# A new order of the instructions, sums by batch ahead of the experts' layers, and 20 products of zeros on TensorE

## The chip, the cores and the metric

The kernel runs on one core of a Trainium2 chip. The metric is the device time of one execution in microseconds (us). The core has four engines that compute, each with its own queue of instructions in program order: TensorE (PE in the rows; PEld is its loading of weights), VectorE (DVE), ScalarE (ACT) and GpSimd (POOL). SyncE (SP) issues the large DMA transfers.

## The reference

An attention with 32 inducing points over four batches of 11456 rows of 128 numbers, and behind it a soft mixture of eight experts with four slots each. Cut to what matters:

```python
def mab(q, kv):
    s = scale * (q @ kv.transpose(0, 2, 1))
    a = softmax(s, -1)
    return a @ kv
h = mab(I, x)                        # 32 x 128 for each batch
x = mab(x, h).reshape(B * N, D)
logits = x @ phi                     # 45824 x 32
slot_input = softmax(logits, 0).T @ x        # over ALL rows of all batches
for e in range(E):
    slot_out[e] = relu(slot_input[e] @ w1[e]) @ w2[e]
out = softmax(logits, 1) @ slot_out
```

The softmax over axis 0 runs over every row of every batch, so the experts' layers can't start until the last row has its logits, and no output can be written until the experts' layers are done.

## The kernel before, in words

The rows are cut into 24 tiles (`n` = 0 to 23, six for each batch), each 128 partitions of 15 rows with 32 scores a row, so a tile of scores is 128 x 480. A tile goes through these steps:

- loads `xn` (rows on the partitions) and `xt` (transposed); for batch 0 `xt` is made on TensorE.
- `first_scores`, `first_max`, `first_sum`, `first_out`: the first attention of a batch, tiles `s1p`, `s`, `e`, `ha`, `h`.
- `second(n)`: the second attention's scores `s2p`, moved to SBUF by DVE (`bts`, tile `bt`), the maximum (`bmx`, tile `bm`), the subtraction on POOL (`bsb`), the exponential on ACT (`bxp`), transposes `tt`, the logits `lp`, and their scaled copy in `l_all` (`ble`, `blf`). POOL scales `bt` by 1/sum (`bml`).
- `segment(k)`: three tiles form one of eight segments (`SEGS`). `h0` (or `blm` for single tiles) takes the column maximum of their logits, `h1` to `h4` spread it over the partitions (tiles `pt`, `mc`, `pb`, and `m_all`), `ds` subtracts it (tile `d`, on DVE for tiles listed in `DV`, on POOL for the others), `de` takes the exponential, and `c2` sums into `u`, 128 x 32 for each segment, which `u1` copies to `us_all`.
- `experts()`: the sums of all segments are brought to one maximum and put through the experts. In `before` the first seven segments are joined early (`e1` to `e7`) and the last one late (`g1` to `g8`). `e5` multiplies each segment's sum with its batch's `h` (tile `sip`). `g9` are the first layer's products (tile `hpm`), `ga`, `gb`, `gc` the relu and the transpose, `gd` the second layer (tile `so`), `ge`, `gf`, `gs` bring the result, divided by the total `rz`, to `srs`. That total comes from POOL (`g4b`, `g4c`, tiles `vs` and `vr`) through a product on TensorE (`g7`, tile `zpp`).
- `third(n)`: the softmax over the 32 columns (`cm`, `ct`, `cz`), which needs no expert, and its transposed copy into `l_all` (`ctr`). `ml` (row `ct<-ct,cz`) is its scaling on POOL, `sb` its subtraction, `hf` a half sum.
- `output(n)`: the products with `srs` (tile `po`), copies to `ot` by ACT or DVE, and the store.

The work of every tile is listed in a `Plan`, but the order in which it is issued is the table `ORDER`, two characters for each operation; it fixes each engine's queue and also in which order buffers of a ring (`RINGS`) are reused. The costs given to `op(...)` don't act on the chip. PSUM tiles come from one ring `mm` of eight.

Of the kernel before, what the change touches and what calls it, by code (L numbers as in the profile page):

```python
# [1063 lines left out]
```

## Time and profile before

| | |
|---|---|
| median of 3 runs | 225.55 us (225.12 to 226.31) |
| profiled execution: its own time | 225.43 us |
| its span, first to last instruction | 223.3 us |
| busy: PE, DVE, ACT, POOL | 189.0, 162.1, 138.1, 124.9 us |
| mean granted TensorE clock | 0.920 of full speed |
| read from and written to HBM | 49.84 MB, 23.59 MB |

Of the profiled execution's time 2.1 us lie outside its span. Busy times are unions of an engine's instructions; a busy TensorE need not be at its peak, since its matmuls overlap.

### The profile page before, as it was taken

How to read it: one execution, taken by the hardware profiler on the slowest of the kernel's cores; microseconds unless marked ns; L12 is line 12 of the kernel's file. 1: busy time of each engine (PE TensorE's matmuls, PEld its weight loads, DVE VectorE, ACT ScalarE, POOL GpSimd, SP SyncE). 2: the span in 40 equal slices, each digit the busy share in tenths (PEclk: the TensorE clock that was granted, in tenths of full speed). 3: DMA queues.
4: the chain of work that ended last, by engine and by line, in shares of the span. 5: the costliest groups of instructions: out<-in, count | busy, mean ns of one | idle time of the engine just before them, and what ended most of it. 6: DMA issues, size and time to landing. Idle time of an engine off the chain costs nothing. (4 is left out here: it accounts for less than half of the span.)

```text
span 223.3 us, 6826 instructions
## 1 busy us (share of the span) xinstructions
PE 189.0 (85%) x2762; PEld 126.0 (56%) x2762; DVE 162.1 (73%) x368; ACT 138.1 (62%) x371; POOL 124.9 (56%) x135
## 2 busy tenths in 40 slices
PE   8899999999999999999998996899879989960000
PEld 8666563687356986348884695788635543510000
DVE  0113867987999989998989899946799999762000
ACT  2587433966465994458966697613299999991000
POOL 0000001586488968588697899977968857610000
PEclk9999999999999999999999999557999999995555
DMA  7999999995999999899999920000079999999994
GB/s 222 406 424 416 418 413 399 422 416 209 312 398 423 414 417 414 302 388 420 414 416 417 409 95 3 0 3 4 4 290 409 417 418 413 415 413 420 421 412 204
DMA packets 12846, 73.87 MB, mean 331 GB/s; under 512 B 1680, under 2 KB 2832, under 8 KB 12816
## 3 DMA queue, kind: packets, MB, share of 16 engines
q1 hardware_dynamic: 12384, 73.27, 81.3%
q8 instruction: 22, 0.36, 0.6%
q10 hardware_dynamic: 432, 0.17, 0.3%
q14 instruction: 8, 0.07, 0.1%
HBM read 49.84 MB, written 23.59 MB: 329 GB/s over the span
## 5 line engine op out<-in xcount | busy, mean ns | idle before, releaser
L941 PE MATMUL po<-l_all,srs 32*128 32x480 f32 x192 | 35.8, 609 | 5.1 <-DVE ot L952 2.8
L952 ACT COPY ot<-po 128x480 f32<-128x480 f32 x67 | 35.1, 679 | 2.8 <-PE po L941 2.8
L568 POOL TENSOR_TENSOR bt<-bt,bm 128x480 f32<-128x480 f32 x24 | 23.7, 1000 | 16.4 <-DVE bm L564 8.1
L941 PEld LDWEIGHTS po<-l_all,srs 32*128 32x128 f32 x192 | 17.2, 183 | 23.1 <-DVE ot L952 10.7
L913 POOL TENSOR_TENSOR ct<-ct,cz 128x480 f32<-128x480 f32 x24 | 23.8, 994 | 6.2 <-DVE cz L532 5.9
L620 POOL TENSOR_TENSOR bt<-bt,bz 128x480 f32<-128x480 f32 x24 | 23.6, 995 | 5.2 <-DVE bz L602 2.7
L326 DVE TENSOR_SCALAR_CACHE_REDUCE s<-s1p 128x480 f32<-128x480 f32 (+1 forms) x24 | 15.2, 644 | 15.5 <-PE s1p L315 15.2
L590 PE MATMUL lp<-bdg,a2t 128*128 128x132 f32 x192 | 25.8, 280 | 0.1
L505 POOL TENSOR_TENSOR ct<-l_all,cm 128x512 f32<-128x512 f32 x20 | 21.0, 1052 | 8.5 <-DVE l_all L916 6.7
L691 POOL TENSOR_TENSOR d<-l_all,m_all 128x512 f32<-128x512 f32 x20 | 22.9, 1166 | 4.4 <-ACT m_all L670 3.2
L590 PEld LDWEIGHTS lp<-bdg,a2t 128*128 128x128 f32 x192 | 23.2, 190 | 3.7 <-ACT a2t L584 1.6
L391 PE MATMUL ha<-xn,e 128*32 128x128 f32 x600 | 21.0, 275 | 0.0
L315 PE MATMUL s1p<-xt,it_sb 128*32 128x480 f32 x160 | 19.9, 573 | 0.7 <-ACT xt L300 0.7
L315 PE MATMUL s2p<-xt,hts 128*32 128x480 f32 x160 | 19.0, 572 | 1.0 <-issue 1.0
L509 ACT ACTIVATE ct<-ct 128x480 f32<-128x480 f32 x24 | 15.7, 661 | 6.6 <-POOL ct L505 5.5
L391 PEld LDWEIGHTS ha<-xn,e 128*32 128x32 f32 x600 | 16.9, 110 | 2.9 <-issue 2.0
L952 DVE COPY ot<-po 128x480 f32<-128x480 f32 x29 | 17.9, 634 | 0.2 <-PE po L941 0.2
L694 ACT ACTIVATE d<-d 128x512 f32<-128x512 f32 x24 | 14.9, 630 | 5.0 <-POOL d L691 2.5
L372 ACT ACTIVATE s<-s,negm 128x480 f32<-128x480 f32 (+1 forms) x24 | 16.4, 685 | 2.4 <-DVE negm L357 2.4
L328 POOL MEMSET s<- 128x16 f32 x4 | 0.5, 113 | 31.1 <-DVE e L375 30.8
L916 DVE STREAM_TRANSPOSE l_all<-ct 128x480 f32<-128x480 f32 x24 | 15.7, 661 | 2.3 <-POOL ct L913 2.3
L561 DVE STREAM_TRANSPOSE bt<-s2p 128x480 f32<-128x480 f32 x24 | 15.7, 666 | 1.7 <-PE u L704 0.9
(126 smaller groups left out, 370.3 us busy)
## 6 DMA issues: line engine op xcount, KB each, us to landing
xn<-xn SPq DMA_DIRECT2D x19, 960.0 KB, 11.6
out<-ot SPq DMA_DIRECT2D x19, 960.0 KB, 8.5
xt<-xt SPq DMA_DIRECT2D x14, 960.0 KB, 14.8
w<-w SPq DMA_DIRECT2D x8, 960.0 KB, 10.7
l_all<-xn SPq DMA_DIRECT2D x4, 960.0 KB, 10.3
l_all<-xt SPq DMA_DIRECT2D x4, 960.0 KB, 13.5
out<-ot SPq DMA_DIRECT2D x6, 480.0 KB, 7.3
out<-ot SPq DMA_DIRECT2D x8, 240.0 KB, 2.5
```

The source lines that it names most:

```text
L315: nc.tensor.matmul(dst[32 * g : 32 * g + 32, :w], lhs, src, start=True, stop=True)
L372: nc.scalar.activation(t[:, :v], t[:, :v], AF.Exp, bias=T["negm", b, g], accum_out=z6[:, a : a + 1])
L391: nc.tensor.matmul(ha[32 * q : 32 * q + 32, :P], T["e1", a][:, j * S : (j + 1) * S], T["xn", a][:, j * P : (j + 1) * P], start=c == lo and ...
L505: nc.gpsimd.tensor_tensor(t.rearrange("p (a e s) -> p a e s", s=S, e=2), l_blocks(n), m, op=ALU.subtract)
L509: nc.scalar.activation(t, t, AF.Exp)
L568: nc.gpsimd.tensor_tensor(t, t, T["bm", n][:, :nb].unsqueeze(2).broadcast_to(full), op=ALU.subtract)
L590: nc.tensor.matmul(pt[:, q * 4 * SZ : (q * 4 + m) * SZ], t[: m * S, q * P : (q + 1) * P], bdgs[b % 2].rearrange("p q s -> p (q s)")[: m * ...
L620: nc.gpsimd.tensor_tensor(t, t, T["bz", n][:, :nb].unsqueeze(2).broadcast_to(full), op=ALU.mult)
L691: e.tensor_tensor(t.rearrange(o, s=S, e=2), l_pairs(n), m, op=ALU.subtract)
L913: nc.gpsimd.tensor_tensor(t, t, T["cz", n][:, :nb].unsqueeze(2).broadcast_to([P, nb, S]), op=ALU.mult)
L941: nc.tensor.matmul(ptile("mm", ("po", 4 * n + g))[:, :w], T["srs",][q, :], l_of(n)[q, :], start=True, stop=True)
L952: (nc.vector.tensor_copy if dve else nc.scalar.copy)(ot[:, g * w : (g + 1) * w], T["po", m][:, :w])
```

## The change

The constants and the code of the changed parts, cut:

```diff
-CHALF = [9, 10, 11, 16]
+CHALF = [9, 10, 11, 12, 16]
 CQ = []
 CB = []
-DV = [12, 20, 21, 23]
+DV = [12, 20, 21, 22, 23]
...
-OD2 = [0, 2, 3, 4, 5, 6, 7, 8, 9, 10, 11, 12, 13, 14, 15, 16, 17, 18, 20, 22, 23]
+OD2 = [0, 2, 3, 4, 5, 7, 8, 9, 10, 11, 12, 13, 14, 16, 17, 18, 20, 21, 22, 23]
...
-NTAG = {3: 'xe', 4: 'xd', 5: 'xc', 18: 'xa'}
-SPLIT = {0: 1, 1: 1, 2: 4, 3: 2, 22: 2, 23: 4, 10: 2}
+NTAG = {3: 'xe', 4: 'xd', 5: 'xc', 18: 'xa', 1: 'xa'}
+SPLIT = {0: 4, 1: 1, 2: 4, 3: 2, 22: 2, 23: 4, 10: 2, 21: 2}
...
+NF = 20
...
+    "000102030406050e070a08090p0b0c0f0d0h0g0A0j0i0l0k0q0w0m0s0r0u0L0t0n0v0x0B0o0y0C0W0H0z0D0F170E180M0G190Q0N3z1a0O0I0S1f0X1i0Z1g130Y1j113D0P1h100R1k120J0T3H140U1l0K1m150V3E163L3A1b1c3I"
...
+K = sum(t < (B - 1) * NCH for t in SEG_AT)
...
-    def warm(key, count):
+    def warm_into(t, count=1):
         for _ in range(count):
-            nc.tensor.matmul(T[key][:, :P], wz, wz, start=True, stop=True)
+            nc.tensor.matmul(t[:, :P], wz, wz, start=True, stop=True)
...
-        K = NSEG - 1
-        last = slice(K * S, NSEG * S)
-        m_last = m_all[:, K * S : (K + 2) * S]
-        m_past = m_all[:, (K + 1) * S :]
+        m_last = m_all[:, K * S :]
+        m_past = m_all[:, NSEG * S :]
+        last = slice((NSEG - 1) * S, NSEG * S)
+        W = NSEG + 1 - K
...
+            o = 4 * ZW + K * S
+            T["ws",] = mb[:, 4 * ZW : o]
+            T["uss",] = mb[:, o : o + K * S]
+            T["usp",] = mb[:, o + K * S : o + (K + B - 1) * S]
...
+        def e6(b):
+            def f():
+                lo, hi = (min(t for t in range(K + 1) if SEG_AT[t] >= NCH * x) for x in (b, b + 1))
+                nc.vector.tensor_reduce(T["usp",][:, b * S : (b + 1) * S], T["uss",][:, lo * S : hi * S].rearrange("p (k s) -> p s k", s=S), axis=AX.X, op=ALU.add)
+            return f
+
...
         def e5():
             sip = ptile("mm", ("sip",))
-            for t in range(K):
-                nc.tensor.matmul(sip[:, :S], T["h", SEG_AT[t] // NCH], T["uss",][:, t * S : (t + 1) * S], start=t == 0, stop=t == K - 1)
+            for b in range(B - 1):
+                nc.tensor.matmul(sip[:, :S], T["h", b], T["usp",][:, b * S : (b + 1) * S], start=b == 0, stop=b == B - 2)
...
-            nc.vector.tensor_reduce(stile("vs", ("vs",), S, 1), T["uss",].rearrange("p (k s) -> p s k", s=S), axis=AX.X, op=ALU.add)
+            nc.vector.tensor_reduce(stile("vs", ("vs",), S, 1), T["usp",].rearrange("p (k s) -> p s k", s=S), axis=AX.X, op=ALU.add)
...
-                blocks(stile("w2", ("wl",), 2 * S, 1)), blocks(m_last), T["nm",].unsqueeze(1).broadcast_to([P, 2, S]), op=ALU.subtract,
+                blocks(stile("w2", ("wl",), W * S, 1)), blocks(m_last), T["nm",].unsqueeze(1).broadcast_to([P, W, S]), op=ALU.subtract,
...
+        def g4a():
+            r = slice(K * S, (NSEG - 1) * S)
+            nc.gpsimd.tensor_tensor(us_all[:, r], us_all[:, r], T["wl",][:, : (W - 2) * S], op=ALU.mult)
+
+        def g4d(k):
+            def f():
+                nc.gpsimd.tensor_tensor(T["vs",], T["vs",], us_all[:, k * S : (k + 1) * S], op=ALU.add)
+            return f
 
...
+        def g6c():
+            for k in range(K, NSEG - 1):
+                nc.tensor.matmul(T["sit",][:, :S], T["h", B - 1], us_all[:, k * S : (k + 1) * S], start=False, stop=False)
...
+        for b in range(B - 1):
+            op("DVE", 0.2, ("e6", b), e6(b), [("uss",), ("mb",)], [("usp", b)])
+        op("PE", 0.3 * (B - 1), ("e5",), e5, [("mb",)] + [(x, b) for b in range(B - 1) for x in ("usp", "h")], [("sip",)], [("mm", ("sip",))], ni=4 * B - 4)
...
+        op("Pool", 0.25 + 0.06 * (W - 2), ("g4a",), g4a, [("wl",)], [("us", k) for k in range(K, NSEG - 1)])
         op("PE", 0.4, ("g6a",), g6a, [("sis",)], [("sit",)], [("mm", ("sit",))], ni=4)
-        op("DVE", 0.1, ("g5",), g5, [("u", K), ("wl",)], [("us", K)])
...
+    def fill(k):
+        def f():
+            warm_into(ptile("mm", ("fill", k)))
+        return f
+
+    for k in range(NF):
+        op("PE", 0.22, ("fill", k), fill(k), [("eps0",)], [("fill", k)], [("mm", ("fill", k))], ni=4)
     T["plan"] = plan
```

`K` is 6 in place of 7: the early join takes the six segments of batches 0 to 2, and the late one the two segments of batch 3. The early sums are added by batch on DVE (`e6`, three instructions, tile `usp` inside `mb`), so `e5` has three products in place of seven. The late join gains a scaling on POOL (`g4a`), an addition on POOL (`g4d`) and a product (`g6c`). Tile 22's subtraction `ds` moves from POOL to DVE, tile 12's third softmax gains a half sum on POOL, the first tile's store is cut otherwise, the load of tile 1 goes to another buffer. Each of the 20 fills is one 128 x 128 product of zeros into a PSUM tile of its own that nobody reads. All other lines of the diff change costs given to `op(...)`, and `ORDER` is a new table.

What the new table does is seen in the queues. On TensorE, from the last segment's maximum (`pb`) to the sums `sit` that feed the experts, the queue before is:

```order
L667 MATMUL pb_2369<-cst,mc_2348 128x32
L772 MATMUL sip<-mb,h_513 128x32 x2
L772 MATMUL sip<-mb,h_1056 128x32 x2
L772 MATMUL sip<-mb,h_1431 128x32 x2
L772 MATMUL sip<-mb,h_2053 128x32
L704 MATMUL u_2404<-d_2376,bt_2057 32x32 x15
L704 MATMUL u_2404<-d_2378,bt_2096 32x32 x15
L704 MATMUL u_2404<-d_2393,bt_2105 32x32 x15
L803 MATMUL sit<-sis,cst 128x32
```

and of the changed kernel (`u_2330` is the sum of segment 6, `u_2427` that of segment 7):

```order
L669 MATMUL pb_2380<-cst,mc_2371 128x32
L225 MATMUL fill_2388<-srs 128x128
L706 MATMUL u_2330<-d_2320,bt_2003 32x32 x15
L225 MATMUL fill_2409<-srs 128x128
L782 MATMUL sip<-mb,h_509 128x32
L782 MATMUL sip<-mb,h_916 128x32
L782 MATMUL sip<-mb,h_1437 128x32
L225 MATMUL fill_2425<-srs 128x128
L706 MATMUL u_2427<-d_2406,bt_2061 32x32 x15
L225 MATMUL fill_2451<-srs 128x128
L822 MATMUL sit<-sis,cst 128x32
L706 MATMUL u_2427<-d_2417,bt_2073 32x32 x15
```

Eleven fills stand ahead of these rows, two of them directly ahead of `pb`, and two stand behind the last `sit`, ahead of `hpm`; the three `sip` products are behind the last `u` products of segment 6 and ahead of those of segment 7, as the seven were.

On DVE, at the last tiles' scores `bts` (`bt<-s2p`), the queue before is (`t_5` is the maximum of segment 5 by `h0`):

```order
L561 STREAM_TRANSPOSE bt_2010<-s2p_1977 128x480
L652 TENSOR_REDUCE t_5_2020<-l_all 128x32
L564 TENSOR_REDUCE bm_2051<-bt_2010 128x15
L561 STREAM_TRANSPOSE bt_2057<-s2p_2005 128x480
L462 TENSOR_TENSOR bdg_89<-gp_2041,cst 128x4x32
L564 TENSOR_REDUCE bm_2074<-bt_2057 128x15
L561 STREAM_TRANSPOSE bt_2096<-s2p_2015 128x480
L561 STREAM_TRANSPOSE bt_2105<-s2p_2046 128x480
L564 TENSOR_REDUCE bm_2113<-bt_2096 128x15
L564 TENSOR_REDUCE bm_2122<-bt_2105 128x15
```

and of the changed kernel:

```order
L563 STREAM_TRANSPOSE bt_2061<-s2p_1987 128x480
L563 STREAM_TRANSPOSE bt_2073<-s2p_1998 128x480
L566 TENSOR_REDUCE bm_2080<-bt_2061 128x15
L566 TENSOR_REDUCE bm_2090<-bt_2073 128x15
L563 STREAM_TRANSPOSE bt_2097<-s2p_2065 128x480
L654 TENSOR_REDUCE t_5_2115<-l_all 128x32
L604 RECIPROCAL bz_2125<-bz_2125 128x15
L566 TENSOR_REDUCE bm_2133<-bt_2097 128x15
```

The maximum `t_5` and one reciprocal moved behind the last `bt<-s2p` and ahead of the last `bm<-bt`.

On POOL, ahead of `vr`, which the total of the softmax waits for, the queue before is:

```order
L517 TENSOR_TENSOR ch_2580<-ct_2533 128x240
L913 TENSOR_TENSOR ct_2490<-ct_2490,cz_2531 128x480
L792 TENSOR_TENSOR vs<-vs,wl 128x32
L517 TENSOR_TENSOR ch_2627<-ct_2548 128x240
L795 TENSOR_TENSOR vr<-vs,us_all 128x128
```

and of the changed kernel:

```order
L811 TENSOR_TENSOR vs<-vs,wl 128x32
L942 TENSOR_TENSOR ct_2495<-ct_2495,cz_2531 128x480
L807 TENSOR_TENSOR vs<-vs,us_all 128x32
L519 TENSOR_TENSOR ch_2587<-ct_2541 128x240
L507 TENSOR_TENSOR ct_2593<-l_all,cm_1925 128x512
L507 TENSOR_TENSOR ct_2629<-l_all,cm_2282 128x512
L519 TENSOR_TENSOR ch_2642<-ct_2593 128x240
L942 TENSOR_TENSOR ct_2541<-ct_2541,cz_2599 128x480
L519 TENSOR_TENSOR ch_2676<-ct_2629 128x240
L814 TENSOR_TENSOR vr<-vs,us_all 128x128
```

Between `vs<-vs,wl` and `vr` there was one half sum `ch`; now there are three, two subtractions `ct<-l_all`, two scalings `ct<-ct` and the new addition.

## Rows read from the trace of the kernel before

**Rows 1.** The page's slices: granted TensorE clock, DMA share, DMA rate, 40 equal slices.
```profile
PEclk9999999999999999999999999557999999995555
DMA  7999999995999999899999920000079999999994
GB/s 222 406 424 416 418 413 399 422 416 209 312 398 423 414 417 414 302 388 420 414 416 417 409 95 3 0 3 4 4 290 409 417 418 413 415 413 420 421 412 204
```
**Rows 2.** Windows: busy time (instructions) of PE, PEld, DVE, ACT, POOL; clock; DMA share, GB/s.
```profile
135.00:140.00 5.00, 3.15 (x147) 2.34 (x149) 5.00 (x12) 3.86 (x11) 5.00 (x6) 1.00 0.01 3
140.00:145.00 5.00, 4.04 (x74) 3.71 (x66) 4.82 (x11) 3.14 (x8) 4.78 (x7) 0.50 0.00 0
...
150.00:155.00 5.00, 5.00 (x113) 4.32 (x109) 2.55 (x6) 1.56 (x4) 4.92 (x7) 0.64 0.01 3
165.00:170.00 5.00, 3.79 (x28) 1.89 (x21) 5.00 (x12) 5.00 (x13) 2.68 (x3) 1.00 1.04 389
```
**Rows 3.** Windows of longer stretches, same columns.
```profile
35.00:140.00 105.00, 101.91 (x1769) 69.52 (x1769) 97.47 (x216) 72.60 (x217) 80.20 (x82) 1.00 0.87 349
163.00:163.50 0.50, 0.50 (x6) 0.33 (x3) 0.50 (x2) 0.50 (x2) 0.50 (x2) 1.00 0.63 223
163.50:220.50 57.00, 32.94 (x173) 15.61 (x170) 34.95 (x70) 37.78 (x88) 23.69 (x24) 0.83 1.01 412
```
**Rows 4.** Chain of waits from the last sums to srs: start, us, what.
```profile
142.59 3.19 PE sip L772 x14
145.79 1.43 PE u L704 x90
...
148.55 5.72 PE hpm L826 x112
...
156.70 2.38 PE so L855 x80
...
160.24 0.35 DVE srs L868
```
**Rows 5.** Timeline of PE at the kernel's start: start, us, what, idle before.
```profile
1.11 3.78 PE L223 MATMUL warm<-srs 128*128 128x128 f32 x16 [1.11 <-DVE srs L219]
```
**Rows 6.** Timeline of DVE, three places.
```profile
55.98 1.74 DVE L652 TENSOR_REDUCE t<-l_all 128x32 f32<-128x1536 f32 x1
...
127.36 0.68 DVE L561 STREAM_TRANSPOSE bt<-s2p 128x480 f32<-128x480 f32 x1 [0.91 <-PE u L704]
127.97 1.17 DVE L564 TENSOR_REDUCE bm<-bt 128x15 f32<-128x480 f32 x2
```
**Rows 7.** Timeline of ACT, the last segment's exponentials.
```profile
143.11 1.88 ACT L694 ACTIVATE d<-d 128x512 f32<-128x512 f32 x3 [0.82 <-DVE d L691]
```
**Rows 8.** Timeline of POOL, 130 to 158 us.
```profile
130.63 2.90 POOL L620 TENSOR_TENSOR bt<-bt,bz 128x480 f32<-128x480 f32 x3
133.49 5.64 POOL L691 TENSOR_TENSOR d<-l_all,m_all 128x512 f32<-128x512 f32 x5
139.09 0.66 POOL L759 TENSOR_TENSOR mb<-m_all 128x224 f32<-128x224 f32 x1
...
143.61 0.32 POOL L781 TENSOR_TENSOR wl<-m_all,nm 128x64 f32<-128x64 f32 x1
...
144.82 1.29 POOL L746 MEMSET ma<- 128x1440 f32 x1
...
149.16 1.05 POOL L505 TENSOR_TENSOR ct<-l_all,cm 128x512 f32<-128x512 f32 x1 [1.14 <-DVE l_all L916]
150.17 0.99 POOL L913 TENSOR_TENSOR ct<-ct,cz 128x480 f32<-128x480 f32 x1
...
154.91 0.25 POOL L792 TENSOR_TENSOR vs<-vs,wl 128x32 f32<-128x32 f32 x1
156.52 0.70 POOL L517 TENSOR_TENSOR ch<-ct 128x240 f32<-128x240 f32 x1 [1.36 <-DVE cz L526]
157.18 0.46 POOL L795 TENSOR_TENSOR vr<-vs,us_all 128x128 f32<-128x128 f32 x1
```

More of the change, by code (lines that the diff above doesn't have):

```diff
@@ L872, in experts @@
         op("Pool", 1.15, ("g0b",), g0b, [wk[2][0]], [("z2", 1), ("ws",), ("uss",)], [("x", ("mb",))])
-        op("DVE", 0.3, ("e1",), e1, [("mk", k) for k in range(K)], [("mp",)])
+        op("DVE", 0.33, ("e1",), e1, [("mk", k) for k in range(K)], [("mp",)])
         op("Pool", 0.6, ("e2",), e2, [("mp",), ("mb",)] + [("mk", k) for k in range(K)], [("ws",)])
@@ L876, in experts @@
         op("Pool", 0.6, ("e4",), e4, [("ws",), ("mb",)] + [("us", k) for k in range(K)], [("uss",)])
-        op("PE", 0.3 * K, ("e5",), e5, [("uss",), ("mb",)] + [("h", SEG_AT[k] // NCH) for k in range(K)], [("sip",)], [("mm", ("sip",))], ni=4 * K)
-        op("DVE", 0.3, ("e7",), e7, [("uss",), ("mb",)], [("vs",)])
-        op("DVE", 0.1, ("g1",), g1, [("mk", K), ("mp",)], [("nm",)])
-        op("Pool", 0.3, ("g2",), g2, [("nm",), ("mk", K), ("mp",)], [("wl",)])
-        op("ACT", 0.14, ("g3",), g3, [], [("wl",)])
@@ L882, in experts @@
-        op("DVE", 0.09, ("g4",), g4, [("wl",), ("sip",)], [("sis",)])
+        for b in range(B - 1):
+            op("DVE", 0.2, ("e6", b), e6(b), [("uss",), ("mb",)], [("usp", b)])
+        op("PE", 0.3 * (B - 1), ("e5",), e5, [("mb",)] + [(x, b) for b in range(B - 1) for x in ("usp", "h")], [("sip",)], [("mm", ("sip",))], ni=4 * B - 4)
+        op("DVE", 0.2, ("e7",), e7, [("mb",)] + [("usp", b) for b in range(B - 1)], [("vs",)])
+        op("DVE", 0.15, ("g1",), g1, [("mk", k) for k in range(K, NSEG)] + [("mp",)], [("nm",)])
@@ L883, in experts @@
+        op("Pool", 0.35, ("g2",), g2, [("nm",), ("mp",)] + [("mk", k) for k in range(K, NSEG)], [("wl",)])
+        op("ACT", 0.16, ("g3",), g3, [], [("wl",)])
+        op("DVE", 0.11, ("g4",), g4, [("wl",), ("sip",)], [("sis",)])
+        op("Pool", 0.25 + 0.06 * (W - 2), ("g4a",), g4a, [("wl",)], [("us", k) for k in range(K, NSEG - 1)])
         op("PE", 0.4, ("g6a",), g6a, [("sis",)], [("sit",)], [("mm", ("sit",))], ni=4)
-        op("DVE", 0.1, ("g5",), g5, [("u", K), ("wl",)], [("us", K)])
@@ L901, in experts @@
                 op("PE", 0.244 * len(es), ("gd", k, es[0]), gd(k, es), [("z2", k), ("ma",), ("mb",)] + wk[2], [("so",)], [] if k or es[0] else [("mm", ("so",))], ni=16 * len(es))
[L902 removed]
+        op("DVE", 0.21, ("ge",), ge, [("so",)], [("sos",)])
         op("PE", 0.4, ("gf",), gf, [("sos",)], [("sr",)], [("mm", ("sr",))], ni=4)
[L904 removed]
+        op("DVE", 0.26, ("gs",), gs, [("sr",), ("rz",)], [("srs",)])
     def third(n):
```

94 lines of the change are left out of this document (46 added, 48 removed).

## The prediction

> **What bounds the kernel now.** I read the slices first: the DMA is full while the inputs come in, idle for some 33 us in the middle, and full again to the end [rows 1]. The last stretch is a drain: from 163.5 to 220.5 us the DMA share is 1.01 at 412 GB/s [rows 3], which is 23.5 of the 23.59 MB written. No engine can shorten it. The kernel's end is therefore the first store plus a constant. The first store's data start to move between 163.0 and 163.5 [rows 3], behind `srs`, which ends at 160.24 + 0.35 = 160.59 us [rows 4]. A microsecond won ahead of `srs` is a microsecond of the kernel, as long as the copies keep ahead of the drain; ACT and DVE, which make them, are busy 37.78 and 34.95 of its 57 us [rows 3], so there is room. All of the change is judged by when `srs` ends.
>
> The chain of waits says what lies ahead of it [rows 4]: `sip` from 142.59, the last `u`, the experts' first layer `hpm` from 148.55, the second layer `so` to 156.70 + 2.38 = 159.08, and 1.51 us from there to the end of `srs`. Much of that ran at half clock: the granted clock is 1.00 up to 140 us, 0.50 from there, and in 150 to 155 us it averages 0.64 [rows 2], so it was back at 1.00 for (0.64 - 0.50) / 0.50 = 28% of that window, from about 153.6. These are TensorE's levels of 2.4 and 1.2 GHz. The price is visible in the products themselves: `hpm` took 5.72 / 112 = 51 ns each, nearly all at half clock, `so` 2.38 / 80 = 29.8 ns at full [rows 4]. Ahead of the fall, in 135 to 140, PE was busy 3.15 of 5 us [rows 2]. In the long stretch before, 35 to 140 us, DVE is the engine to watch: busy 97.47 of 105 us, idle 7.53, while POOL has 24.8 us idle [rows 3].
>
> **Sums by batch.** Seven `sip` products show as 14 records, 3.19 us, 228 ns a record at half clock [rows 4]. Three products are six records: 1.4 us at half clock, 0.7 at full. They stand ahead of the last `u`, so up to 2.5 us could come off, but the last `u` also need the last three exponentials, which end at 143.11 + 1.88 = 144.99 [rows 7]. That caps it at about 0.8 us (145.79 against 144.99), and the DVE queue decides what of it is left, below. The three additions on DVE have no row of before; by the smallest and the largest neighbour, a `bm` maximum of 480 numbers at 1.17 / 2 = 0.58 us [rows 6] bounds one from above, zero from below; for 64 numbers I take 0.2, and they lie in the wait between `mc` and the last `pb`, where before two `cm` maxima lay.
>
> **The fills.** At the kernel's start the same product of zeros took 3.78 / 16 = 236 ns a record [rows 5]. A fill is two records: 0.47 us at that price, 0.24 if that stretch ran at half clock, which the slices don't show. `so` against `hpm` differ by a factor of 51 / 29.8 between the two levels, so I take 0.24, and 20 are 4.7 us of PE. Where they stand PE was waiting (1.85 us in 135 to 140 alone [rows 2]). Two stand ahead of `hpm`, 0.47 us, where PE waits for the copy `ma` anyway; their cost is between 0 and 0.47, and I take 0.1. If that cover is gone, it is 0.47. What they can buy is the clock. With it held, 128 records of `hpm` take 128 x 29.8 = 3.8 us against 5.72 + 16 x 29.8 ns = 6.2 before.
>
> Does the clock hold? Ahead of the fall PE was busy 3.15 of 5 us; in 165 to 170 it was busy 3.79 and the clock stayed at 1.00 [rows 2]. The nine fills that now stand in the former stretch are 2.1 us of PE work, as much as the 1.85 us that were idle, and eight more (1.9 us) are strewn through 140 to 147.5, where the real work at full clock is some 4 us. No row tells what is enough; I take it that the clock holds as the likelier. The Trainium skill speaks against part of this: its page "TensorE: Matmul & The Clock Gate", section "A second HAM failure mode: psum-queue depth-cycling", tells of a kernel whose clock swung because PE idled in small gaps between groups of products. By that page the small gaps that remain between fills would still cost the clock, which is the third case below; the fall at 140 here agrees with it, since no wait of PE ahead of it was a long one (1.85 us in all, in several pieces).
>
> **From the last scores to hpm.** On DVE the last `bt<-s2p` ends at 127.36 + 0.68 = 128.04 [rows 6]. I leave that time where it is: counted through the two queues, DVE has ahead of it one `bm` (0.58) and three `cm` (0.6 each, estimated from `bm`) more and one segment maximum (1.74 [rows 6]) less, +0.6 us, and one first score maximum more (480 numbers, 0.6 too) is done in the first 33 us, where DVE waits, so the two cancel. Behind it, up to the last segment's `mc`, the segment maximum is new, and one `bm` and one `cm` are gone: +0.5 us. The last exponential began at 144.99 - 1.88 / 3 = 144.36 [rows 7], so the last `d` had ended by then. Its three `d` are all on DVE now, with that half microsecond ahead of them and a shorter sum between; I put their end at 144.6. Five short DVE rows follow (`sis`, a sum, `vs`, a transposed copy, a reciprocal: 0.15 + 0.6 + 0.2 + 0.6 + 0.2, the long ones after the `bm` and `bt` rows, the short ones estimated), the scaling of `u` at 146.4, then `sit` and `ma`: 1.0 us, where the chain before needed 148.55 - 147.22 = 1.33 with its products at half clock. `hpm` starts at 147.5, 1.05 earlier.
>
> **The experts' layers.** `hpm` ends at 147.5 + 0.1 + 3.8 = 151.4. Both transposes now stand behind all of `hpm`, so that the relu of the second half, its transpose and the copies are no longer covered: 0.7 us, estimated at a quarter each with the waits between. `so` runs from 152.1 to 155.9. That path would end 3.2 us earlier than before.
>
> **POOL.** The second path to `srs` is the total: `vr` on POOL, then `zpp`, which stands ahead of `sr` on PE. Before, `vr` ended at 157.18 + 0.46 = 157.64, 1.4 us ahead of the last `so` [rows 4, 8]. In the new queue everything from the last subtraction `bsb` to `vr` is: six `bt` scalings (2.90 / 3 each, 5.8), five `d` (5.64), two `mb` (0.66 each for 224 numbers, 0.6 for 192: 1.2), `wl` 0.35, the zeroing of `ma` 1.29, three rows of 32 numbers (0.25 each, two of them new: 0.75), four `ct` scalings (0.98 each: 3.9), four `ct` subtractions (1.05 each: 4.2), three `ch` (0.70 each: 2.1) and `vr` 0.46 [rows 8]: 25.7 us. Before it was 157.64 - 130.63 = 27.0, with 2.5 us of waits in the rows shown [rows 8]. The last `bsb` can start only when the last `bm` is there, now behind the segment maximum: 128.04 + 1.7 + 0.2 + 0.6 = 130.5, so it ends at 131.5, 0.9 later than the 130.63 of before. Without waits `vr` ends at 131.5 + 25.7 = 157.2; with the old 2.5 us of waits at 159.7. I take it without: each `ch` and each scaling has two or more other POOL rows ahead of it, longer than the exponential or the sum that it needs.
>
> So the total now ends last: `vr` at 157.2 against `so` at 155.9. From `vr` to `srs` come `zpp`, two short DVE rows and `srs`; the 1.51 us from `so` to `srs` is the nearest row and holds one copy more, so 1.3. `srs` ends at 158.5, **2.1 us earlier**. The new cut of the first stores makes the second tile wait for all four of its copies: I give 0.2 back. The profiled execution would be 225.43 - 1.9 = 223.5; the median of before lies 0.12 above that execution, so **223.6 us**. Bounds: the clock lost costs one more microsecond, the old waits on POOL 2.5.
>
> **The rivals.** The first case is this sum, 222.4 to 224.4.
>
> Second, the new order also wins in the long stretch. It moves every queue from the start on, and 7.53 us of DVE idle time are there to win [rows 3]; against it, PE, DVE, ACT and POOL all have the same work, within about a microsecond, ahead of the last logits as before. With 2.5 us of idle time won it is 221.1.
>
> Third, the clock falls all the same. `hpm` then takes 6.2 us from 147.6, `so` ends at 147.6 + 6.2 + 0.7 + 3.8 = 158.3, `srs` at 159.8: 0.8 earlier, 0.2 given back, 224.9, no change that can be told. For it: eight fills are spread over 7.5 us.
>
> Fourth, on the other side, POOL's chain starts late. 25.7 us of POOL work without a gap hang on the last `bsb`, and that hangs on one DVE row which stands behind the segment maximum. If the last `bt<-s2p` comes 1.9 us later than now, at 129.9, nothing is left of the gain; with over 3.0 us it is slower by over 0.5%. For it: the DVE's idle time in 35 to 140 is as easily lost as won when all is re-ordered, and any wait inside the chain adds to it. With 4 us late it is 227.6.
>
> **How the numbers follow.** About 0.5% (1.1 us) is what a measurement of this kernel can tell from no change: faster is under 224.4, slower over 226.7. First case 0.50, second 0.18, third 0.12, fourth 0.20. Of the first 0.48 is faster, the second all, the third 0.01; the fourth is slower by over 0.5% in 0.14, in between in 0.06. So faster 0.67, same 0.19, slower 0.14. The range from 220.5 to 226.8 leaves out some 0.06 below and 0.13 above.
>
> **What would show it.** In the profile after: granted clock 1.00 from 135 to 160; `hpm` near 30 ns a record; six `sip` records under 1 us; `vr` ending 0 to 1 us before 157.6 with POOL without a gap from the last `bsb`; `zpp` waiting for `vr`, not `sr` for `sos`; `srs` at 158.5; the drain again at 412 GB/s and share 1.0 over 57 us. The forecast is wrong if the last `bt<-s2p` has moved by over 1 us either way, if the clock shows 0.50 during `hpm`, or if the drain has holes.

## The result and the profile after

The changed kernel takes **219.74 us** (median of 4 runs, 218.96 to 220.13) against 225.65 before (4 runs): ratio 0.973, 95% interval 0.970 to 0.977, 5.9 us less. The forecast was 223.6 with a range down to 220.5: the direction held, the size didn't. The profiled execution took 220.13 us, 2.0 of them outside its span of 218.1.

The page's slices of the changed kernel (granted clock, DMA share, rate) answer to [rows 1]:

```profile
PEclk9999999999999999999999999999999769997555
DMA  7999999997799999939999991000099999999995
GB/s 227 391 427 419 414 420 415 402 419 303 244 414 421 418 419 414 371 93 423 419 414 417 413 413 71 3 5 6 5 392 411 414 424 385 403 413 421 414 423 231
```

The dip of the clock in the middle is gone. Its windows, columns as in [rows 2, 3]: PE, PEld, DVE, ACT, POOL, clock, DMA.

```profile
35.00:140.00 105.00, 101.66 (x1806) 73.95 (x1805) 99.83 (x223) 72.57 (x222) 82.16 (x85) 1.00 0.87 349
135.00:140.00 5.00, 4.95 (x117) 4.01 (x116) 5.00 (x11) 3.20 (x8) 5.00 (x7) 1.00 0.01 3
140.00:145.00 5.00, 4.99 (x155) 4.43 (x158) 4.44 (x14) 2.30 (x6) 5.00 (x7) 1.00 0.01 3
150.00:155.00 5.00, 4.62 (x128) 4.04 (x120) 3.74 (x12) 2.08 (x5) 5.00 (x7) 1.00 0.01 3
158.30:215.30 57.00, 36.51 (x174) 20.43 (x170) 33.40 (x68) 37.69 (x88) 23.18 (x24) 0.80 1.01 410
```

POOL is busy without a gap in all three short windows, and the drain is the same one (share 1.01, 410 GB/s over 57 us). The timeline of DVE, at the last scores and at the end of the chain (start, us, row, idle time before):

```profile
125.16 0.67 DVE L563 STREAM_TRANSPOSE bt<-s2p 128x480 f32<-128x480 f32 x1
125.76 1.71 DVE L654 TENSOR_REDUCE t<-l_all 128x32 f32<-128x1536 f32 x1
...
151.54 0.69 DVE L498 TENSOR_REDUCE cm<-l_all 128x16 f32<-128x512 f32 x1 [0.33 <-POOL ct L507]
...
152.99 0.25 DVE L534 RECIPROCAL cz<-cz 128x15 f32<-128x15 f32 x1 [0.37 <-ACT cz L531]
153.16 0.68 DVE L945 STREAM_TRANSPOSE l_all<-ct 128x480 f32<-128x480 f32 x1
153.76 0.25 DVE L885 COPY sos<-so 128x128 f32<-128x128 f32 x1
...
155.13 0.35 DVE L891 TENSOR_SCALAR srs<-sr,rz_l 128x128 f32<-128x128 f32 x1
```

The last `bt<-s2p` ends at 125.83, in [rows 6] at 128.04; `srs` at 155.48, in [rows 4] at 160.59. The first difference isn't one trace's chance: in the nine traces that have the new order up to this row (this one and, of the runs below, e1, e3, e4, e5, e7, e12, e14, e15) it ended between 125.10 and 126.29, in the four with the old order (before, e2, e6, e8) between 127.43 and 128.88. PE between them, and POOL's queue at its two ends (POOL has no idle time noted between the rows shown):

```profile
140.71 0.75 PE L782 MATMUL sip<-mb,h 128*128 128x32 f32 x6
144.66 0.95 PE L849 MATMUL hpm<-w,ma 128*32 128x128 f32 x25
145.88 3.04 PE L849 MATMUL hpm<-w,ma 128*32 128x128 f32 x103 [0.26 <-issue]
151.34 1.93 PE L878 MATMUL so<-w,mb 128*32 128x128 f32 x64
154.25 0.38 PE L833 MATMUL zpp<-ones,vr 128*128 128x1 f32 x2 [0.34 <-POOL vr L814]
```
```profile
128.28 0.99 POOL L570 TENSOR_TENSOR bt<-bt,bm 128x480 f32<-128x480 f32 x1
129.23 1.95 POOL L622 TENSOR_TENSOR bt<-bt,bz 128x480 f32<-128x480 f32 x2
...
153.75 0.44 POOL L814 TENSOR_TENSOR vr<-vs,us_all 128x128 f32<-128x128 f32 x1
```

`hpm` ran at full clock (30 ns a record against 51), and `zpp` waits for `vr`, as forecast; all of it lies some 3 us earlier than forecast.

### The profile page after: what moved, and what is told of

It is laid out like the page before. It is cut to its first block, busy times and chain, and to the rows that moved or that the text cites. A ratio compares the mean times of both kernels' runs of the same rounds, so it can differ in the third digit from the quotient of the medians.

```text
span 218.1 us, 6897 instructions
## 1 busy us (share of the span) xinstructions
PE 186.9 (86%) x2796; PEld 130.5 (60%) x2796; DVE 162.2 (74%) x371; ACT 137.2 (63%) x372; POOL 124.1 (57%) x137
## 4 chain that ended last, share of the span: by engine, by line
PE 40%; DVE 18%; DMA 13%; POOL 9%; ACT 5%; issue 3%; ACTq 1%; SPq 0%; DVEq 0%
PE po L970 11%; DMA xt<-xt 9%; PE ha L393 9%; PE lp L592 7%; PE s2p L317 5%; ACT ot L981 3%; DVE s L328 3%; PE tt L579 3%; DVE bt L563 3%; DVE bm L566 2%; POOL bt L622 2%; DMA phi_sb<-phi 2%; DMA out<-ot 2%; PE s1p L317 2%; POOL ct L507 2%
## 5 line engine op out<-in xcount | busy, mean ns | idle before, releaser
L970 PE MATMUL po<-l_all,srs 32*128 32x480 f32 x192 | 39.2, 671 | 1.1 <-DVE srs L891 0.6
L970 PEld LDWEIGHTS po<-l_all,srs 32*128 32x128 f32 x192 | 21.8, 199 | 18.0 <-ACT ot L981 10.9
L693 POOL TENSOR_TENSOR d<-l_all,m_all 128x512 f32<-128x512 f32 x19 | 21.7, 1165 | 6.4 <-ACT m_all L672 5.8
L592 PE MATMUL lp<-bdg,a2t 128*128 128x132 f32 x192 | 25.1, 278 | 0.1
L393 PE MATMUL ha<-xn,e 128*32 128x128 f32 x570 | 19.7, 275 | 2.4 <-issue 2.2
L317 PE MATMUL s1p<-xt,it_sb 128*32 128x480 f32 x160 | 19.4, 571 | 1.3 <-ACT xt L302 1.1
L573 ACT ACTIVATE bt<-bt 128x480 f32<-128x480 f32 x24 | 14.6, 609 | 7.5 <-POOL bt L570 7.4
L393 PEld LDWEIGHTS ha<-xn,e 128*32 128x32 f32 x570 | 16.2, 109 | 4.1 <-issue 3.2
L377 DVE STREAM_TRANSPOSE e<-s 128x480 f32<-128x480 f32 x24 | 15.5, 664 | 2.6 <-ACT s L374 1.8
L981 DVE COPY ot<-po 128x480 f32<-128x480 f32 x28 | 17.0, 630 | 0.6 <-PE po L970 0.5
```

The lines of the kernel that those rows point to most:

```text
L317: nc.tensor.matmul(dst[32 * g : 32 * g + 32, :w], lhs, src, start=True, stop=True)
L393: nc.tensor.matmul(ha[32 * q : 32 * q + 32, :P], T["e1", a][:, j * S : (j + 1) * S], T["xn", a][:, j * P : (j + 1) * P], start=c == lo and ...
L592: nc.tensor.matmul(pt[:, q * 4 * SZ : (q * 4 + m) * SZ], t[: m * S, q * P : (q + 1) * P], bdgs[b % 2].rearrange("p q s -> p (q s)")[: m * ...
L693: e.tensor_tensor(t.rearrange(o, s=S, e=2), l_pairs(n), m, op=ALU.subtract)
L970: nc.tensor.matmul(ptile("mm", ("po", 4 * n + g))[:, :w], T["srs",][q, :], l_of(n)[q, :], start=True, stop=True)
L981: (nc.vector.tensor_copy if dve else nc.scalar.copy)(ot[:, g * w : (g + 1) * w], T["po", m][:, :w])
```

## The experiments

Three theories of where the 5.9 us come from: **A**, two gains that add up, one in the long stretch (by the order alone) and one behind it; **B**, all behind the last scores (clock, POOL's queue); **C**, all in the long stretch. Ratios are to the kernel before, run beside each.

### Seams: the order of one kernel up to a row, of the other behind it

```diff
-ORDER = one
+head = other[: other.index(cut) + 1]
+ORDER = head + [x for x in one if x not in head]
```

**e1** and **e2** cut at the last `bt<-s2p` (with before's code and its order behind in e1; the changed kernel's in e2).

> The new order up to the last bt<-s2p, and behind it the old order with the old experts' code (seven segments, no fills). Theory A (two parts: about 2.2 us from the last bt<-s2p coming earlier, about 3 us from the stretch behind it): last bt<-s2p at about 126, half clock behind 138 as in the kernel before, about 223.4 us. Theory B (the fills and the held clock are the whole gain, the earlier scores would be lost in waits behind them): 225.6. Theory C (the new order ahead of the last scores is the whole gain): 220.

> The old order up to the last bt<-s2p, and behind it all of the new one with sums by batch and 20 fills. Theory A: last bt<-s2p at 128, vr some 25.5 us behind the last bsb, srs at about 157.5, 222.5 us. Theory B: 220. Theory C: 225.6.

Measured: e1 226.03 us, ratio 1.000 (0.997 to 1.004); e2 224.37, 0.992 (0.989 to 0.994). Taken at face value neither part explains the gain. The timeline of e1's PE at the seam shows why that reading would be wrong:

```profile
127.81 0.27 PE L657 MATMUL pt<-cst,t 128*32 128x128 f32 x1 [2.28 <-DVE t L652]
127.92 1.72 PE L590 MATMUL lp<-bdg,a2t 128*128 128x132 f32 x8
```

At this cut the two orders have not done the same work. In e1 the transpose of a segment maximum that DVE has only begun now stands ahead of the logits' products, and PE stands still for 2.28 us; e1's last `bt<-s2p` was at 126.02, as early as in the changed kernel, and its last `l_all` of a tile 1.7 us later than before (139.56 against 137.88). The seam ate what the head had won. In e2 POOL stands at its seam, 1.98 us for a `bm`. **e5** and **e6** repeat the split at the seventh `mc`, where the two orders differ by three rows.

> The order of the changed kernel up to the seventh segment's maximum mc (there 133.59 us, before 135.70), and behind it the code and the order of the kernel before: no fills, sums by segment, the last segment alone at the end. In the first attempt at this split the seam itself cost 3.2 us of DVE waits behind the last bt<-s2p; at this seam the two orders have done the same work but for three rows. Theory A (two gains that add up: about 2.1 us from the long stretch, about 3.8 behind it): mc at 133.6, srs 2.1 us earlier than before, 224.2, ratio 0.991. Theory B (all of it lies behind the seam): no change, 226.3, ratio 1.000. Theory C (all of it lies ahead): about 220, ratio 0.974.

> The complement: the order of the kernel before up to the seventh mc (135.70 us), and behind it the changed kernel's code and order, with the fills and the sums by batch. Theory A: mc at 135.7, and the stretch from there to srs is as short as in the changed kernel (155.48 - 133.59 = 21.9 us against 24.9 before), so srs at 157.6, 3.0 us earlier than before, 223.2, ratio 0.987. Theory B: 220, ratio 0.974. Theory C: 226.3, ratio 1.000.

Measured: e5 223.38, 0.990 (0.986 to 0.993); e6 223.15, 0.989 (0.984 to 0.993). That is theory A: 2.5 and 2.8 us, each near its number, and B and C fall. In e6 the number was met by two deviations: its `mc` ended at 135.09 in place of 135.7, and from there to `srs` it took 22.9 us, a microsecond more than expected. The product of the ratios is 0.978; the whole change's 0.973 lies within the intervals of it. In e5 the clock fell again (0.50 in 145 to 150), in e6 it stayed at 1.00, so the clock belongs to the second part alone.

**e9, e10, e11** ask where in the long stretch the first part is won, with before's order up to 33, 72 and 115 us.

> The order of the kernel before up to the first batch's product hp (about 33 us in; at that seam the two orders have done the same work but for one row), and the changed kernel's code and order behind it; tile 1's place in memory is as before too. It asks where in the long stretch the 2.2 us by which the last bt<-s2p came earlier were won. Counted by DVE's idle time in the two traces, with the 0.6 us of work that the new order adds there: 0.7 us in the first 35 us, 1.7 between 35 and 65, -1.3 between 65 and 100, +1.7 between 100 and 128. If this bookkeeping holds: last bt<-s2p 0.7 us later than in the changed kernel (126.5), 220.4, ratio to before 0.976. If the start decides all of it (the loads and their order): 222, ratio 0.983. If the start gives nothing: 219.8, ratio 0.973.

> The same with the seam at the 18th first score's maximum (72.88 us in the kernel before, 71.59 in the changed one). By the bookkeeping of DVE's idle time 2.4 us of gain lie ahead of this seam, 1.1 of which the new order gives back behind it: last bt<-s2p at 127 to 128, 221 to 222, ratio 0.979 to 0.983. If what counts is won behind 100 us alone: 219.8, ratio 0.973.

> The same with the seam at tile 13's subtraction d (about 115 us), six rows apart. By the bookkeeping only the last 0.9 + 0.6 us of DVE's waits (for u and for m_all, in the kernel before at 127 and 118 us) are still to be won behind this seam: last bt<-s2p at 127, 221.5 to 222.5, ratio 0.981 to 0.985. If the whole of the long stretch's gain lies ahead of it, the result is that of the seam at the seventh mc: 223.2, ratio 0.989.

Measured: e9 220.17, 0.975 (0.972 to 0.978); e10 224.40, 0.996 (0.993 to 0.998); e11 222.17, 0.985 (0.982 to 0.988). e9 keeps the gain: its last `bt<-s2p` ended at 126.10, within the spread of the new order, so neither the order of the first 33 us nor the new place of tile 1's load, which e9 takes back, gives anything that shows. e10 and e11 don't settle the question: their last `bt<-s2p` ended at 130.50 and 129.07, later than in either order unmixed, so these seams have waits of their own. In e10 PE stood 3.06 us for an exponential of ACT shortly behind the seam, and the granted clock was 0.84 and 0.82 in 75 to 80 and 80 to 85 us. e11's time met its number, but its `bt<-s2p`, expected at 127, did not.

### What paces the long stretch

**e13**: the kernel before, with seven rows of DVE's queue that waited moved behind rows that were ready. Two of the places:

```diff
-L443 TENSOR_SCALAR rz_768<-hp_750 128x1
-L444 RECIPROCAL rz_768<-rz_768 128x1
 L496 TENSOR_REDUCE cm_768<-l_all 128x16
 L526 TENSOR_REDUCE cz_778<-ct_748 128x15
+L443 TENSOR_SCALAR rz_780<-hp_750 128x1
+L444 RECIPROCAL rz_780<-rz_780 128x1
...
-L602 RECIPROCAL bz_1634<-bz_1634 128x15
 L357 TENSOR_REDUCE negm_0_1652<-pm_0_1636 128x1
 L564 TENSOR_REDUCE bm_1654<-bt_1606 128x15
+L602 RECIPROCAL bz_1634<-bz_1634 128x15
```

> The kernel before with seven rows of DVE's queue each moved behind one to three rows that were ready earlier, and nothing else: the reciprocal rows rz of three batches, one reciprocal of cz and one of bz, one d, and the last bt<-s2p. In the trace of before DVE waited 1.06, 0.36, 0.60, 0.38, 0.73, 0.43 and 0.91 us at these rows, 4.5 us in all. Theory A, that DVE's waits are what the new order saved in the long stretch: the last bt<-s2p ends 2 to 3 us earlier than 128.04 and the kernel takes 223 to 224, ratio 0.988 to 0.993. Rival: another engine sets the pace there (PE is busy nearly throughout), the waits come back at other rows, and the time stays at 225.7, ratio 1.000.

Measured: 226.17, 1.000 (0.997 to 1.003). The rival holds as far as DVE goes: 4.5 us of waits were moved out of the way and nothing came of it. From 35 us to the end of the last `bt<-s2p`, itself one of the moved rows and now at 129.60, DVE was idle 8.51 us, against 7.54 before. The timeline of e13's DVE has the waits at the neighbours:

```profile
50.89 0.69 DVE L496 TENSOR_REDUCE cm<-l_all 128x16 f32<-128x512 f32 x1 [0.77 <-ACT l_all L616]
53.54 0.25 DVE L602 RECIPROCAL bz<-bz 128x15 f32<-128x15 f32 x1 [1.14 <-ACT bz L598]
...
104.16 0.16 DVE L357 TENSOR_REDUCE negm<-pm 128x1 f32<-128x4 f32 x1 [1.03 <-PE pm L354]
...
119.17 0.25 DVE L602 RECIPROCAL bz<-bz 128x15 f32<-128x15 f32 x1 [0.98 <-ACT bz L598]
```

So DVE's idle time there is a symptom: taking waits out of its queue alone wins nothing. **e16, e17, e18** load one engine each in the kernel before:

```diff
-            col_mm(ptile("mm", ("s2p", n)), T["hts", b], n)
+            t = ptile("mm", ("s2p", n))
+            if 2 <= n < 22:
+                nc.tensor.matmul(t[:, :P], wz, wz, start=True, stop=True)
+            col_mm(t, T["hts", b], n)
```
```diff
+            for _ in range(2 if n in (3, 5, 8, 10, 13, 15, 18, 20) else 1):
+                nc.vector.tensor_reduce(t[:, :nb], blocks(a2_of(n)), axis=AX.X, op=ALU.max)
```
```diff
+            for _ in range(1 if n not in (2, 4, 6, 8, 10, 12, 14, 16, 18, 20) else 2):
+                nc.scalar.copy(t[:, :o], pt[:, :o])
```

> The kernel before with one product of zeros ahead of each of the second scores' products s2p of tiles 2 to 21, into the same place, which the real product then overwrites: 20 products at 0.236 us a record, 40 records, up to 9.4 us of PE work by the records and half that if the two records of a product overlap, spread over 37 to 123 us. If PE sets the pace of the long stretch: 3 to 5 us slower, 229 to 231, ratio 1.013 to 1.022. If DVE does, and PE has room between: 226 to 226.5, ratio 1.000 to 1.002.

> The kernel before with the maximum bm taken twice for eight tiles (3, 5, 8, 10, 13, 15, 18, 20), the second time into the same place: 8 rows of 0.58 us, 4.6 us of DVE work spread over 43 to 124 us. If DVE sets the pace: 3 to 4.6 us slower, 229 to 230.5, ratio 1.013 to 1.020. If PE does: some of it is lost in the chain from bm to the exponential, under 1.5 us, ratio under 1.007. If each engine holds the other up in turn, both probes cost between 1.5 and 3 us.

> The kernel before with the copy a2t of ten tiles (2, 4, ... 20) done twice, the second time into the same place: ten rows of 0.47 us, 4.7 us of ACT work spread over 41 to 120 us. ACT is busy 60.5 of 90 us in 35 to 125, so by its share of busy time it has room: 226 to 227, ratio 1.000 to 1.005. If the stretch is paced by the chains through the engines (a product, a copy, a product) rather than by one engine's load, a row of ACT in that chain costs as much as one of PE or DVE: 2 us or more, ratio over 1.009.

Measured: e16 233.29, 1.033 (1.025 to 1.040); e17 228.62, 1.012 (1.005 to 1.020); e18 229.67, 1.017 (1.010 to 1.024). The group of e16's added products:

```profile
L560 PE MATMUL s2p<-srs 128*128 128x128 f32 x39 | 9.1, 313 | 0.0
```

9.1 us more on PE cost 7.9 us, more than the 3 to 5 expected. Eight rows of DVE (0.62 each, 5.0 us) cost 3.2, the lower edge of "DVE sets the pace"; ten of ACT (0.48 each, 4.8 us) cost 4.3. The last `bt<-s2p` ended 8.4, 3.4 and 4.3 us later than before, so the cost arises in this stretch. For a microsecond added that is 0.87, 0.64 and 0.90, and by the intervals of the ratios the three can't be told apart. So the probes single out no engine: a row added on any of the three costs most of its length, even on ACT, which is idle a third of the time (72.60 of 105 us busy in [rows 3]). That fits closed chains through several engines, a product, a copy and a product that wait for each other in turn; no run tests the chains themselves. ACT's price holds a part of the clock: in e18's trace PE stood 2.19 us shortly before 120.6, and a window there shows

```profile
120.00:125.00 5.00, 4.40 (x53) 2.35 (x56) 2.16 (x4) 2.74 (x9) 2.32 (x3) 0.66 1.01 413
```

At most (1.00 - 0.66) x 5 = 1.7 of the 4.3 us can be that, an estimate from this row.

### The parts behind the last scores

**e3**: the changed kernel without the fills (`NF = 0`). **e8**: the kernel before with 20 fills at the places that answer to them.

```diff
-NF = 20
+NF = 0
```
```diff
+    for k in range(NF):
+        op("PE", 0.22, ("fill", k), fill(k), [("eps0",)], [("fill", k)], [("mm", ("fill", k))], ni=4)
```

> The changed kernel without the 20 fills, all else in the same order. Theory A: the clock falls to 0.50 near 138 us, hpm at 51 ns a record, the path over so ends at about 156.3 in place of 153.3 and takes over from vr, srs 2.3 us later: 222. Theory B: all of the gain is lost, 225.6. Theory C, or a clock that holds without them: 219.7.

> The kernel before with 20 products of zeros on PE at the places that answer to those of the changed kernel; all else as before. Theory A: the granted clock stays at 1.00 through 140 to 155, hpm and so take about 3.8 us each, so ends some 3 us earlier, and then vr at 157.6 binds: srs at 158.9, 1.7 us earlier, 224.6, ratio 0.992. If the fills are worth the same microsecond as they were in the changed kernel: 225.4, ratio 0.996. If they stand in PE's way as much as they bring: 226.3, ratio 1.000.

Measured: e3 220.60, 0.978 (0.972 to 0.984); e8 224.47, 0.993 (0.991 to 0.996). e3's windows in the profiled execution, which took 222.98:

```profile
135.00:140.00 5.00, 3.17 (x103) 2.26 (x107) 5.00 (x11) 3.12 (x8) 5.00 (x7) 0.70 0.02 3
140.00:145.00 5.00, 4.95 (x132) 4.58 (x132) 3.98 (x12) 2.41 (x7) 4.97 (x7) 0.50 0.01 3
145.00:150.00 5.00, 4.67 (x86) 4.22 (x89) 3.85 (x8) 1.64 (x4) 3.93 (x6) 0.50 0.02 5
150.00:155.00 5.00, 4.85 (x150) 4.28 (x146) 2.50 (x7) 1.87 (x6) 4.17 (x5) 0.93 0.01 3
```

Without fills PE is busy 3.17 of 5 us and the clock falls, as before; `srs` ended at 157.58, 2.1 us later than with them. Its four executions took 222.98, 220.98, 220.00 and 220.22 us at a mean clock of 0.903, 0.910, 0.932 and 0.925, which suggests that the fall doesn't always last as long; only the first has a trace, and these means take in the drain, whose clock isn't 1.00 either. With fills the mean was 0.941 to 0.947 in all four. Against the changed kernel's median the fills are worth 0.3 to 3.2 us in these executions, 0.9 by the medians, and the intervals of the two ratios overlap; e8's gain, 1.45 us by the medians, is clear of noise. In e8 the clock was 1.00 from 135 to 160 us, `so` ended at 157.0 and `srs` at 159.00, 1.6 us earlier than before, where the expectation had 1.7. Its reason did not hold: `vr`, which was to bind, ended at 156.34, ahead of `so`.

**e14**: the changed kernel with `sip` by segment and no sums by batch.

```diff
-            for b in range(B - 1):
-                nc.tensor.matmul(sip[:, :S], T["h", b], T["usp",][:, b * S : (b + 1) * S], start=b == 0, stop=b == B - 2)
+            for t in range(K):
+                nc.tensor.matmul(sip[:, :S], T["h", SEG_AT[t] // NCH], T["uss",][:, t * S : (t + 1) * S], start=t == 0, stop=t == K - 1)
...
-        for b in range(B - 1):
-            op("DVE", 0.2, ("e6", b), e6(b), [("uss",), ("mb",)], [("usp", b)])
```

> The changed kernel without the sums by batch: sip has six products by segment, 12 records, and the three short additions on DVE ahead of the last d are gone. If the sums by batch matter: six more records at 125 ns, 0.75 us, ahead of the last u on PE, and hpm 0.5 us later, 220.3, ratio 0.976. If they are hidden, as POOL's queue ends as late as so: 219.8, ratio 0.973. If the additions on DVE stood in the way of the last d: 219.4.

Measured: 220.01, 0.973 (0.969 to 0.976). The sums by batch are worth nothing that shows: `sip` took 1.42 us in place of 0.75, `hpm` started 0.5 us later, and `vr` ended at 154.2 all the same.

**e7** puts tile 22's `d` back on POOL, **e4** moves `vr` ahead in POOL's queue.

```diff
-DV = [12, 20, 21, 22, 23]
+DV = [12, 20, 21, 23]
```
```diff
 L807 TENSOR_TENSOR vs<-vs,us_all 128x32
+L814 TENSOR_TENSOR vr<-vs,us_all 128x128
 L519 TENSOR_TENSOR ch_2587<-ct_2541 128x240
...
 L519 TENSOR_TENSOR ch_2676<-ct_2629 128x240
-L814 TENSOR_TENSOR vr<-vs,us_all 128x128
```

> The changed kernel with tile 22's subtraction d back on POOL (1.13 us there, 0.68 on DVE). The forecast's step under test is that the total of POOL's queue sets the end. If POOL's queue to vr binds: vr at 155.3, srs at 156.6, about 1.1 us later than in the changed kernel, 220.8, ratio to before 0.978. If the experts' products bind and vr only happens to end close to them: 219.8, ratio 0.973; and if the later d delays the last u, and with it hpm, over 221.

> The changed kernel with one POOL row moved: vr directly behind the last addition to vs, ahead of three half sums, two subtractions and one scaling, which end 0.46 us later. Theory A (vr, on POOL, ends last): vr at about 149.5, srs set by so, 0.5 to 0.7 us earlier, 219.1. Theory B (TensorE's path sets srs): no change or 0.1 us slower, 219.8.

Measured: e7 220.99, 0.980 (0.974 to 0.986), 1.2 us more for 1.17 us of POOL work; e4 220.01, 0.974 (0.970 to 0.977), nothing, though `vr` began at 148.16 in place of 153.75. Together they look like a contradiction: POOL's length counts in full, `vr` itself doesn't. The rows of e4 resolve it, DVE's first and then PE's:

```profile
151.35 0.69 DVE L498 TENSOR_REDUCE cm<-l_all 128x16 f32<-128x512 f32 x1 [0.33 <-POOL ct L507]
...
152.80 0.25 DVE L534 RECIPROCAL cz<-cz 128x15 f32<-128x15 f32 x1 [0.38 <-ACT cz L531]
152.97 0.68 DVE L945 STREAM_TRANSPOSE l_all<-ct 128x480 f32<-128x480 f32 x1
153.58 0.25 DVE L885 COPY sos<-so 128x128 f32<-128x128 f32 x1
```
```profile
150.60 1.93 PE L878 MATMUL so<-w,mb 128*32 128x128 f32 x64
...
153.89 0.49 PE L888 MATMUL sr<-sos,cst 128*128 128x128 f32 x2 [0.59 <-DVE sos L885]
```

`so` ended at 152.53, but its copy `sos` stands on DVE behind rows of a third score (`cm`, `cz`, a transpose) that hang on POOL's `ct`, and began only at 153.58; `sr` and `srs` then wait for it. And `vr`, 0.46 us long, now stands ahead of that `ct` on POOL. Counted from the last `bt<-s2p` (125.10 in e4), `cm` began at 26.25 us in e4 and 25.71 in the changed kernel, `sos` at 28.48 and 27.93, and `srs` ended at 29.85 and 29.65. In e7 both paths moved by the same amount: counted so, `vr` and `sos` each lie 1.1 us later. Both paths to `srs` hang on POOL's queue, at different places of it; taking `vr` off frees only one.

### A version that frees both

**e12**: `vr` early, `htm` of the first half within `hpm`, its copy `ma` ahead of a third score's transpose that waits for POOL, `zpp` in the middle of `so`, `sos` and `srs` ahead of such transposes, two fills fewer. **e15**: the same, with one of these transposes ahead of `srs` again and the first copies `ot` ahead of third-score rows.

```diff
 L878 MATMUL so<-w_2223,ma 32x128 x4
+L833 MATMUL zpp<-ones,vr 128x1
 L878 MATMUL so<-w_2063,mb 32x128 x5
...
 L498 TENSOR_REDUCE cm_2575<-l_all 128x16
+L867 COPY ma<-htm_2570 128x32x4
 L945 STREAM_TRANSPOSE l_all<-ct_2495 128x480
-L867 COPY ma<-htm_2589 128x32x4
```
```diff
+L981 COPY ot_2706<-po_2713 128x480
+L981 COPY ot_2706<-po_2709 128x480
 L511 ACTIVATE ct_2701<-ct_2701 128x480
-L981 COPY ot_2709<-po_2716 128x480
-L981 COPY ot_2709<-po_2712 128x480
```

> The changed kernel with both of the paths to srs shortened at once: vr on POOL directly behind the last row of 32 numbers; the transpose htm of the first half between the two parts of the second half of hpm, its copy ahead of a ct transpose on DVE, the second half's transpose between the two parts of so's first half; zpp in the middle of so; sos directly behind the sum that is in its way least, srs ahead of the ct transpose of tile 9; the last two fills left out. Theory: with vr alone early the path over so and sos was 0.5 us behind it, so that only both together can pay: so starts at 148.4 in place of 149.3, sos no longer waits 0.6 us behind a ct transpose, srs ends about 1.5 us earlier than in the changed kernel, 218.3, ratio 0.967. If a third path is as close as these two (the copies ahead of the first stores, or the drain itself), nothing moves: 219.8, ratio 0.973.

> e12 with the rows behind srs put right: the ct transpose of tile 9 ahead of srs again (in e12 POOL waited 0.87 us for it), the first copies ot on ACT ahead of an exponential that waits for POOL, the first one on DVE ahead of two rows of the third scores. In e12 srs ended at 154.32 in place of 155.48, yet the first store was issued at 157.14 in place of 157.33, and the drain had holes. Theory: the copies behind srs took its place; with them in front the first store goes out 1 us earlier, 218.6 to 219.2, ratio 0.969 to 0.972. If the work of the third scores, late by the same amount, holds up the drain instead: 220 to 221.7, ratio 0.975 to 0.983.

Measured: e12 221.72, 0.983 (0.980 to 0.986); e15 221.00, 0.974 (0.970 to 0.978). Both miss: e12 is some 2 us slower than the changed kernel, e15 no faster. Of the 1.2 us by which e12's `srs` (154.32) is earlier, 0.65 had been there already at the last `mc` (138.55 against 139.20), so the stretch itself is 0.5 us shorter, in e15 0.4. And more than that is lost behind it: from the end of `srs` to the end of the profiled execution the changed kernel needs 220.13 - 155.48 = 64.65 us, e12 66.43, e15 65.53. PE's timeline in e12 shows one half of it, the second tile's products waiting for buffers of the first:

```profile
154.37 1.89 PE L970 MATMUL po<-l_all,srs 32*128 32x480 f32 x16 [0.45 <-DVE srs L891]
158.29 1.09 PE L970 MATMUL po<-l_all,srs 32*128 32x480 f32 x8 [2.02 <-DVE ot L981]
```

e15 mends that half (first store 1.87 us behind `srs`, as in the changed kernel, against 2.82 in e12); the other stays, with 405 GB/s over the 57 us of the drain against 410. It would fit that work of the third scores, pushed back for `srs`, comes due in the drain; no run separates this from the rest.

## Why the prediction was wrong

**The step that failed** is "I leave that time where it is": the last `bt<-s2p`, forecast at 128.04, ended at 125.83. The rest of the chain was counted from it, so 2.2 us went straight into the result; it is also the prediction's own sign of being wrong, a move "by over 1 us either way". e5 shows that the order alone brings this part, ahead of the seventh `mc`. The step failed because it counted rows in DVE's queue, "so the two cancel", as if DVE set the pace. [rows 3] had shown otherwise: in 35 to 140 us PE was busy 101.91 of 105 us, DVE 97.47. e16 to e18 show for the kernel before that a row of PE or ACT costs there as much as one of DVE, as far as the intervals tell, and e13 that taking waits out of DVE's queue alone wins nothing. Nor was DVE's row count a bound: a queue that waits for others can end earlier with the same rows. The windows from 35 us to the end of the last `bt<-s2p`, of the kernel before and then of the changed one, show it:

```profile
35.00:128.04 93.04, 91.79 (x1565) 60.66 (x1562) 85.50 (x189) 62.65 (x186) 68.93 (x70) 1.00 0.96 387
```
```profile
35.00:125.83 90.83, 87.61 (x1561) 61.48 (x1561) 85.66 (x192) 61.15 (x186) 68.09 (x70) 1.00 0.94 377
```

DVE has the same work, 85.5 and 85.7 us, and 7.54 and 5.17 us of idle time.

**POOL's total was too long.** The sum was 25.7 us from the last `bsb` to `vr`; it took 154.19 - 129.27 = 24.9, without a wait, as chosen. The 0.8 us are overlaps: each row reaches some 0.04 us into the next (128.28 + 0.99 = 129.27 above, where the next starts at 129.23), and the sum added full lengths. The way to the last `bsb` (3.44 us behind the last `bt<-s2p`, forecast 3.46) and from `vr` to `srs` (1.29, forecast 1.3) were right.

**The end.** 0.2 us were to be lost in the first stores; instead the rest of the execution was 0.2 shorter than before (64.65 against 225.43 - 160.59 = 64.84). So 2.2 + 0.8 + 0.4 = 3.4 us make up the distance from the forecast execution, 223.5, to the measured one, 220.13; the medians lie 0.5 further apart.

**Right:** the bound by POOL's queue (e7), the clock held by the fills (e8, e3), the length of `hpm` and its cover. Right for a reason that was incomplete: `so` ended 2.2 us ahead of `srs` and was not the bound, but its copy `sos` hangs on the same queue (e4). **Mis-sized without effect:** a fill was priced at 0.24 us, half of what the product took at the kernel's start; by the prediction's own factor of 51 / 29.8 it would have been 0.28. Its two records last 0.275 us each: five fills in a row took 1.38 us, 0.28 each, a fill alone 0.49, and all 20 made PE busy for 6.97 us in place of 4.7. PE had the room: in 135 to 140 it was busy 4.95 of 5 us with them, 3.17 without (e3). The sums by batch were given up to 0.8 us on the way to `hpm`; e14 shows 0.5 there and none at the end.

**The rivals.** The second case, "the new order also wins in the long stretch", with 2.5 us of DVE's idle time and 221.1 us, is what happened, on top of the first. It had a chance of 0.18. For the third, the clock stayed at 1.00 with fills, also where small gaps were left between them (PE busy 4.62 of 5 us in 150 to 155); without fills it fell (e3, 3.17 of 5 us busy in the window of the fall). The Trainium skill ("TensorE: Matmul & The Clock Gate", section "A second HAM failure mode: psum-queue depth-cycling") tells of a kernel in which small gaps between groups of products cost the clock. The fall in e3 agrees with it; the gaps left between the fills, in 150 to 155, cost no clock here. The fourth, a late POOL chain, had the right place and the wrong sign.

**What stays open** is which rows of the new order win the 2.2 us. No run exchanges the queue of one engine alone, and the seams inside the stretch added waits of their own. That PE shows 87.61 busy us in place of 91.79 for nearly the same products is a hint and no proof, since the ends of its products are modelled. Behind the seventh `mc`, the fills (0.9 us by the medians of e3), tile 22's subtraction on DVE (1.2, e7) and the sums by batch (nothing, e14) were taken away singly; which rows bring the rest of e6's 2.8 us was not run.
